# Attention over two heads at once: 64-row score products and transposes, float32 values in 64-column halves, minimum taken while scores leave PSUM

## The chip, the cores and the metric

The kernel runs on one core of a Trainium2 chip, in one launch. The metric is device time in microseconds (us), the median of the runs. The engines are TensorE (PE; its weight loads are listed apart as PEld), VectorE (DVE), ScalarE (ACT), GpSimd (POOL) and SyncE (SP, which issues most DMAs). A matrix product loads a stationary operand into the array and streams the columns of the moving operand past it; results land in PSUM, eight banks of 512 float32 per partition.

## The reference, cut to what matters

Two batches of eight heads, 1152 positions, head size 64. Queries are averaged in pairs, so that 576 queries meet 1152 keys. Two gated feed-forward layers follow.

```python
# q, k, v: (2, 8, 1152, 64) float32
q_pool = q.reshape(B, H, S // 2, 2, D).mean(axis=3)              # 576 queries
scores = scale * np.matmul(q_pool, k.transpose(0, 1, 3, 2))
scores = scores - np.max(scores, axis=-1, keepdims=True)
attn = np.exp(scores)
attn = attn / (np.sum(attn, axis=-1, keepdims=True) + 1e-09)
x = np.matmul(attn, v)                                          # heads side by side: (1152, 512)
g = x @ w_gate                                                  # 512 -> 1536
x = (g / (1 + np.exp(-g)) * (x @ w_val)) @ w_out                # -> 512
h = x @ w_in                                                    # 512 -> 2048
out = (np.maximum(h, 0) + alpha * np.minimum(h, 0)) @ w_out2    # -> 512
```

## The kernel before, in words

**Precision.** TensorE takes two kinds of 32-bit operand here. In the rounded kind (F32R) one product is one pass. To keep float32 accuracy the kernel splits an operand into a rounded high part and the rest (hi and lo) and adds hi*hi, lo*hi and hi*lo. A product of plain float32 is a second way.

**Attention, one pair of heads at a time** (NP = 8 pairs; the loop at L710). The two heads of a pair lie on partitions 0 to 63 and 64 to 127. `prep` (L418) loads q, k and v, pools and splits q (`qsplit`) and splits k (`ksplit`), mostly on POOL. Then SP copies, by DMA inside SBUF (L524, L526), the hi and lo parts of each head under one another, so that one product over 128 rows does two of the three terms (`qq`, `kk`). POOL splits v (L542, L543) and puts hi and lo side by side, 128 columns for a head.

A pair has nine units of 128 query rows (`unit`, L557): four of the first head, four of the second, and unit 4, which holds the last 64 queries of both heads by a block-diagonal operand `bd`. In a unit the scores (negated) are built in three cuts of 448, 448 and 256 keys (L592), two products a cut (three for unit 4). DVE takes the minimum of the first two cuts (L601) and then of the third together with it (L602); ACT does the exponential from PSUM into SBUF with the sum of the row (L604, L606). `transposed` (L615) turns the unit's nine blocks of 128x128 on TensorE (L633), three to a PSUM bank. Each bank is split again: the high part by ACT (L655), the rest by DVE (L656); 8 of 27 blocks go instead through an ACT copy (L641) to POOL (L651, L652). `values` (L661) then streams the hi and lo parts of 256 or 320 queries past v, 18 products of 128 columns for each of four groups (L674), and ACT and DVE add the two halves of the result (L678, L679). `inverses` (L681) turns the row sums into a multiplier that travels over DRAM, and `finish` (L694) multiplies and splits the result into `xh` and `xl`.

**The first pair** starts before the splits exist: its first two units use plain float32 q and k on 64 rows (the terms with `x.raw`), and the other units of its first head use three 64-row products per cut, straight from `qhl` and `khl`. Matmuls of zeros (L294) fill TensorE's time until attention flows.

**Feed-forward.** `gated` and `out1`, `prelu` and `out2` (L762, L822, L851) are products of 384 or 512 columns, three terms each, with weights rebuilt from 64-bit words by `weights` (L377).

**Order.** A planner (`Plan.run`, L124) writes out the order of every engine at build time, from fixed costs (`mm`, `tp`, `act`, `dve`, `gp`) and priorities (KNOB), with a due order by pair and unit. Buffers are classes of slots. PSUM before: banks 0 and 1, and 3 and 4, for the two wide cuts; bank 2 for the third; 5, 6 and 2 for transposes (`t`); 7 for values (`acc`). The feed-forward products (`b`) take any bank, but only when the attention classes that share it are all done.

Of the kernel before, what the change touches and what calls it, by code (L numbers as in the profile page):

```python
# [17 lines left out]
P = 128  # L18
# [3 lines left out]


KNOB = dict(hold_0=0.177, hold_m=0.061, qadd=0, qhi=1, klo=3, first=-4, raw=2, ramp=9, qk0=-2.332, max0=-0.894, exp0=0.979, t0=-3, hi0=-0.64, lo0=-0.532, v0=-3, last=2, qk9=-2.161, exp9=-1.953, t9=-0.316, hi9=0.54, lo9=1.303, v9=0.71, pool9=2, pooln=6, wlo=1, qk=-1.58, max=-1.852, exp=-0.223, t=-0.504, hi=-0.646, lo=-1.72, v=1.568, prep=-0.146, fin=1.131, hold_pe=0, hold_act=0.259, hold_dve=0.048, hold_pool=0.096, pvn=1, begin=0, lead=2, floor=31.257, warm=8, wide=448, tb=(5, 6, 2), ab=(7,), pool=9, xl=0, e=3, et=6, wc=3, wr=4, h=17)


class Task:
    __slots__ = ("eng", "dur", "extra", "emit", "prio", "bufs", "left", "after", "ready", "start", "n", "done", "port", "late", "hold")
# [12 lines left out]
class Slot:  # L41
    __slots__ = ("ap", "cells", "buf", "after")


class Plan:
# [3 lines left out]
    LAT = {PE: 0.21, ACT: 0.15, DVE: 0.13, POOL: 0.1, SP: 0.05}  # L49

# [9 lines left out]
    def place(self, cls, slots, after=()):  # L60
# [3 lines left out]
        for ap, cells in slots:  # L64
            s = Slot()
            s.ap, s.cells, s.buf = ap, frozenset(cells), None
            s.after = [o for o in after if any(s.cells & x.cells for x in self.classes[o]["slots"])]
            made.append(s)
# [11 lines left out]
    def add(self, eng, dur, emit, prio, reads=(), writes=(), bufs=(), extra=0.0, port=False, late=0.0, hold=0.0):  # L80
        t = Task()
        t.eng, t.dur, t.extra, t.emit, t.prio = eng, dur, extra, emit, prio
        t.n = len(self.tasks)
        t.port, t.late = port or eng == POOL, late
# [39 lines left out]
    def run(self, hold):  # L124
# [5 lines left out]
        port = 0.0  # L130
        events, seq = [], 0

# [4 lines left out]

        for when in sorted(set(free.values())):
            event(when)
        for t in self.tasks:  # L140
            if not t.left:
                heapq.heappush(wait[t.eng], (t.prio, t.n, t))
        order = []
        while events:
# [7 lines left out]
            for e in free:  # L152
                if free[e] > now + 1e-9:
                    continue
                passed = []
                while wait[e]:
                    item = heapq.heappop(wait[e])
                    t = item[2]
                    if t.ready > now + 1e-9:
                        passed.append(item)  # L160
                        if t.ready <= now + max(hold[e], t.hold) and all(b.slot is not None or self._spot(b) for b in t.bufs):
# [768 lines left out]
```

## Time and profile before

| | |
|---|---|
| Median of 3 runs | 686.75 us (680.51 to 686.88) |
| Span of the profiled execution | 685.0 us |
| Instructions | 11099 |
| PE busy | 676.4 us (99%) |
| DVE, ACT, POOL busy | 519.0, 392.2, 219.2 us |

The profiled execution is given by its span, from its first to its last instruction; the runs' times also hold what lies around that. Busy time of PE counts matmuls from start to modelled end, so PE at 99% says only that something was always in flight. What a product costs is read from the distance between starts, which the chain of waits shows (each piece there is a number of instructions and the time they took in the chain).

### The profile page before, as it was taken

What the parts mean: (1) busy time and instruction counts of PE and PEld (TensorE: products, weight loads), DVE (VectorE), ACT (ScalarE), POOL (GpSimd) and SP (SyncE); (2) the same over time, 40 slices, a digit from 0 to 9 for tenths busy, and PEclk for the clock granted to TensorE, in tenths of its full rate; (3) what the DMA queues carried; (4) which work ended last, traced back from release to release, by engine and by line L of the source; (5) the groups of instructions that cost most, each with busy time, mean ns of one, the idle gap of its engine ahead of it and who ended that gap; (6) DMA issues with size and microseconds to landing.
All of it is one profiled execution on the core that took longest, in us unless ns stands there. A gap on an engine that the chain in (4) does not pass through costs nothing.

```text
span 685.0 us, 11099 instructions
## 1 busy us (share of the span) xinstructions
PE 676.4 (99%) x4073; PEld 633.5 (92%) x4073; DVE 519.0 (76%) x893; ACT 392.2 (57%) x833; POOL 219.2 (32%) x253
## 2 busy tenths in 40 slices
PE   9999999999999989999999999999999999999998
PEld 5888999999999879999999999999999998999886
DVE  3788898888888799999775696559799559653432
ACT  3888999999999985545443432331376464242210
POOL 4668898988989840000000000004100000000000
PEclk9999999999999999999999999999999999999999
DMA  6576384755746324534341122111313303000012
GB/s 154 142 190 190 79 221 100 191 144 127 199 107 144 118 81 140 172 136 147 137 149 62 62 93 95 59 63 62 122 62 124 123 0 124 1 0 1 1 46 93
DMA packets 21431, 72.99 MB, mean 107 GB/s; under 512 B 3128, under 2 KB 3776, under 8 KB 21376
## 3 DMA queue, kind: packets, MB, share of 16 engines
q1 hardware_dynamic: 21296, 72.16, 35.5%
q8 instruction: 32, 0.52, 0.3%
q14 instruction: 23, 0.19, 0.1%
q10 hardware_dynamic: 80, 0.11, 0.1%
HBM read 52.17 MB, written 2.40 MB: 80 GB/s over the span
## 4 chain that ended last, share of the span: by engine, by line
PE 89%; DVE 5%; ACT 2%; issue 2%; DMA 1%; SPq 0%; POOL 0%; DVEq 0%; ACTq 0%
PE bank L762 34%; PE bank L851 14%; PE bank L822 11%; PE bank L592 11%; PE bank L633 9%; PE bank L674 9%; PE bank L294 1%; DMA fed<-fed 1%; DVE fed L656 1%; ACT plain L606 1%; DVE stats L601 1%; DVE magnitudes L393 0%; ACT fed L655 0%; DVE magnitudes L394 0%; DVE junk L602 0%
## 5 line engine op out<-in xcount | busy, mean ns | idle before, releaser
L762 PE MATMUL bank<-xh,weights 128*128 128x384 f32 x960 | 253.9, 337 | 0.1
L762 PEld LDWEIGHTS bank<-xh,weights 128*128 128x128 f32 x960 | 174.5, 188 | 2.1 <-DVE plain L786 0.4
L762 PE MATMUL bank<-xl,weights 128*128 128x384 f32 x480 | 161.4, 336 | 0.0
L633 PE MATMUL bank<-ident,plain 128*128 128x128 f32 x648 | 100.8, 275 | 3.9 <-DVE fed L656 3.0
L674 PE MATMUL bank<-fed 128*128 128x256 f32 (+1 forms) x576 | 104.2, 307 | 0.0
L851 PE MATMUL bank<-fed 128*128 128x512 f32 (+1 forms) x444 | 102.7, 383 | 0.0
L592 PE MATMUL bank<-fed 128*128 128x448 f32 (+2 forms) x378 | 98.5, 360 | 0.2 <-DMA fed<-fed 0.2
L851 PEld LDWEIGHTS bank<-fed 128*128 128x128 f32 x444 | 81.4, 188 | 14.3
L656 DVE TENSOR_TENSOR fed<-bank,fed 128x384 fp32r<-128x384 f32 (+1 forms) x177 | 82.7, 496 | 15.0 <-ACT fed L655 13.6
L762 PEld LDWEIGHTS bank<-xl,weights 128*128 128x128 f32 x480 | 90.2, 188 | 1.0
L633 PEld LDWEIGHTS bank<-ident,plain 128*128 128x128 f32 x648 | 74.8, 140 | 16.2 <-DVE fed L656 5.5
L601 DVE TENSOR_REDUCE stats<-bank 128x1 f32<-128x896 f32 x72 | 78.1, 1085 | 13.5 <-PE bank L592 12.3
L674 PEld LDWEIGHTS bank<-fed 128*128 128x128 f32 x576 | 83.0, 189 | 2.1 <-DVE plain L679 1.1
L655 ACT ACTIVATE fed<-bank 128x384 fp32r<-128x384 f32 (+1 forms) x177 | 73.3, 452 | 16.7 <-PE bank L633 16.2
L822 PE MATMUL bank<-fed 128*128 128x384 f32 x432 | 79.0, 336 | 0.0
L831 POOL TENSOR_SCALAR xh<-plain 128x384 fp32r<-128x384 f32 x12 | 12.1, 1010 | 205.2 <-DVE plain L829 205.2
L822 PEld LDWEIGHTS bank<-fed 128*128 128x128 f32 x432 | 75.8, 188 | 0.0
L606 ACT ACTIVATE plain<-bank,stats 128x896 f32<-128x896 f32 x72 | 72.6, 1009 | 0.0
L802 ACT ACTIVATE plain<-bank,signs 128x384 f32<-128x384 f32 x48 | 27.9, 581 | 69.6 <-PE bank L762 69.4
L652 POOL TENSOR_TENSOR fed<-plain,fed 128x384 fp32r<-128x384 f32 x63 | 64.7, 1027 | 1.5
L592 PEld LDWEIGHTS bank<-fed 128*128 128x128 f32 (+1 forms) x378 | 60.5, 189 | 3.2 <-issue 0.9
L803 DVE SCALAR_TENSOR_TENSOR plain<-bank,signs,plain 128x384 f32<-128x384 f32 x48 | 29.5, 614 | 35.0 <-ACT plain L802 35.0
(77 smaller groups left out, 842.1 us busy)
## 6 DMA issues: line engine op xcount, KB each, us to landing
fed<-fed SPq DMA_DIRECT2D x60, 288.0 KB, 5.4
plain<-in_w_out SPq DMA_DIRECT2D x28, 512.0 KB, 4.2
plain<-in_w_in SPq DMA_DIRECT2D x16, 512.0 KB, 4.1
plain<-in_w_gate SPq DMA_DIRECT2D x12, 512.0 KB, 3.7
plain<-in_w_val SPq DMA_DIRECT2D x12, 512.0 KB, 4.6
plain<-in_vt SPq DMA_DIRECT2D x8, 576.0 KB, 5.5
plain<-in_qt SPq DMA_DIRECT2D x7, 576.0 KB, 7.9
plain<-in_kt SPq DMA_DIRECT2D x7, 576.0 KB
```

What stands on the lines that cost most here:

```text
L592: nc.tensor.matmul(out(i)[:, :js.stop - js.start], l(), r(js), start=a == 0, stop=a == len(terms) - 1)
L601: add(DVE, dve(2 * WIDE), lambda: nc.vector.tensor_reduce(m(1), two(), AX.XY, ALU.min), pos + turn("max", p, n), [(sa, 0), (sa, 1)], [(st, ...
L606: add(ACT, act(2 * WIDE, acc=True), lambda: nc.scalar.activation(e.ap[:, :2 * WIDE].rearrange("p (a b) -> p a b", a=2), two(), AF.Exp, bia ...
L633: nc.tensor.transpose(t.ap[:, c * P:c * P + P], e.ap[:, ks:ks + P], ident)
L652: add(POOL, gp2(BLK * w), lambda cp=cp, to=to, cols=cols: nc.gpsimd.tensor_tensor(to(1), src3(cp.ap)[:, :, cols], to(0).bitcast(F32), ALU. ...
L655: add(ACT, act(BLK * w), lambda t=t, to=to, cols=cols: nc.scalar.activation(to(0), src3(t.ap)[:, :, cols], AF.Copy), at + turn("hi", p, n) ...
L656: add(DVE, dve(BLK * w), lambda t=t, to=to, cols=cols: nc.vector.tensor_tensor(to(1), src3(t.ap)[:, :, cols], to(0).bitcast(F32), ALU.subt ...
L674: nc.tensor.matmul(acc.ap[:, :n], v, b.ap[:, at:at + n], start=kc == 0 and part == 0, stop=kc == NK - 1 and part == 1)
L762: nc.tensor.matmul(acc.ap[:, :TB], l[:, cs], r[:, c, ts], start=c == 0 and a == 0, stop=c == KC - 1 and a == 2)
L803: add(DVE, dve(TB) + 0.056, lambda: nc.vector.scalar_tensor_tensor(u.ap, a.ap[:, :TB], sign(), u.ap, ALU.mult, ALU.max), prio, [a], [u], [ ...
L822: nc.tensor.matmul(acc.ap[:, :TB], l[:, os_], r, start=n == 0 and m == 0, stop=n == len(g) - 1 and m == 2)
L851: nc.tensor.matmul(acc.ap[:, :width], l, r[:, cols], start=n == 0 and m == 0, stop=n == len(g) - 1 and m == 2)
```

## The change

Attention is rewritten; the feed-forward part keeps its instructions. In the diff `TOP` and `LOW` are partitions 0 to 63 and 64 to 127 (head 0 and head 1), `CUTS` are three cuts of 384 keys.

- **Scores.** `two` replaces eight of the nine units: it builds 128 queries of both heads together, three 64-row products per cut and head, head 0 on the array's upper 64 rows and head 1 on the lower, in turn, into two PSUM banks. The DMA copies `qq` and `kk` go away. `corner` keeps the block-diagonal unit.
- **Minimum.** One DVE instruction per cut copies the scores to SBUF and takes the running minimum with it (`minimum`). One ACT instruction does the exponential of a whole row of 1152 in place (`exponential`).
- **Transposes.** Each 128x128 block is turned as two 64-row halves, the upper and the lower rows in turn, into two banks. One copy (ACT or DVE, the planner picks) takes three blocks out of PSUM, as plain float32; the hi and lo split of the weights and of v goes away with its POOL work.
- **Values.** Plain float32: v of head 0 is loaded into the array's left 64 columns, v of head 1 into the right 64, each with its own moving operand, in turn; one copy takes the result out. Two groups a pair instead of four.
- **PSUM.** All eight banks are shared: pairs of banks for scores (`s`) and transposes (`t`), single ones for values (`v`) and the corner (`m`). The first four slots of `b` need no longer wait for the attention classes.
- **Planner.** A task can have more than one engine to choose from, and TensorE tasks have a mode (`rows`, `cols`, `full`) with a price for turning from one to another. Emission comes after planning.
- **First pair.** Its first two `two` units use plain float32 q and k, both heads. The filling matmuls of zeros use 64 rows.
- Buffers: `h` 15 in place of 17, one `xs` in place of two, `e` 5 in place of 3; one weight buffer `raw` of its own.

```diff
+    TURN = {("full", "cols"): 0.15, ("cols", "full"): 0.15, ("rows", "full"): 0.15, ("full", "rows"): 0.195, ("rows", "cols"): 0.15, ("cols", "rows"): 0.198}
...
+                if e == PE:
+                    items.sort(key=lambda i: (i[0] + (stay if i[2].mode != mode else 0.0), i[1]))
...
-        nc.tensor.matmul(bank[:, 7, :n], zeros[:, :P], zeros[:, :n], start=True, stop=True)
+        nc.tensor.matmul(bank[:, 6, :n], zeros[TOP, :P], zeros[TOP, :n], start=True, stop=True)
...
-           [("khl", 1, 2 * S), ("qhl", 1, 2 * SQ), ("qq", 2, 2 * SQ), ("kk", 2, S), ("vs", 2, S), ("et", K["et"], 2 * BLK * 320)],
-           [("wr", K["wr"], 4 * DM), ("h", K["h"], 2 * TB)])
+    GROUPS = [(0, 2 * P), (2 * P, SQ)]
+    WIDEST = SQ - 2 * P
+    region("fed", F32R, [("khl", 2, 2 * S), ("qhl", 2, 2 * SQ)], [("wr", K["wr"], 4 * DM)])
...
+    room, kinds = {}, {"et": (F32, K["et"], 2 * BLK * WIDEST), "h": (F32R, K["h"], 2 * TB)}
...
-           [("nat", 2, S), ("vn", 1, S), (None, 1, 8 * DM - 3 * S), ("e", K["e"], S), ("cp", 2 if K["pool"] else 0, BLK * P), ("eo", 2, SQ), ("xs", 2, SQ), ("rr", 1, SQ)],
-           [("raw", 2, 4 * DM), ("tmp", 6, TB), ("part", 1, KC * NT)])
+           [("nat", 2, S), ("vn", 2, S), ("e", K["e"], S), ("xs", K["xs"], SQ), ("rr", 1, SQ)],
+           [("tmp", 6, TB), ("raw", 1, 4 * DM), (None, 1, 256), ("part", 1, KC * NT)])
...
-    OWN = (0, 3)
-    for i, o in enumerate(OWN):
-        plan.place(f"s{i}", [(None, [("ps", o), ("ps", o + 1)])])
-    plan.place("s2", [(bank[:, 2], [("ps", 2)])])
-    plan.place("t", [(bank[:, i], [("ps", i)]) for i in K["tb"]])
-    plan.place("acc", [(bank[:, i], [("ps", i)]) for i in K["ab"]])
-    plan.place("b", [(bank[:, i], [("ps", i)]) for i in range(8)], ("s0", "s1", "s2", "t", "acc"))
+    for cls in "st":
+        plan.place(cls, [(bank[:, i:i + 2], [("ps", i), ("ps", i + 1)]) for i in range(0, 8, 2)])
+    for cls in "vm":
+        plan.place(cls, [(bank[:, i], [("ps", i)]) for i in range(7, -1, -1)])
+    plan.place("b", [(bank[:, i], [("ps", i)]) for i in range(8)], ("s", "t", "v", "m"))
+    for s in plan.classes["b"]["slots"][:K["early"]]:
+        s.after = []
...
+            qload("a", s0, SP, slice(0, n0))
+            kload(0, s0, ACT)
+            kload(1, s0, SP)
+            kload(2, s0, ACT)
+            qload("b", s0, SP, slice(n0, SQ))
...
-        for j in range(1 if first else 0, 2):
-            qq, kk = buf("qq"), buf("kk")
-            x.qq[j], x.kk[j] = qq, kk
-            src = slice(0, D) if j == 0 else slice(D, P)
-            pr = s0 + 0.5 + 2 * j
-            for a in range(2):
...
-            add(POOL, gp(SQ), lambda v3=v3, vn=vn, hi=hi: nc.gpsimd.tensor_scalar(v3(hi), vn(), 1.0, 1.0, ALU.mult, ALU.mult), pr, [x.vn], [(vs, 0)], [x.vn, vs])
-            add(POOL, gp2(SQ), lambda v3=v3, vn=vn, hi=hi, lo=lo: nc.gpsimd.tensor_tensor(v3(lo), vn(), v3(hi).bitcast(F32), ALU.subtract), pr, [x.vn, (vs, 0)], [(vs, 1)], [x.vn, vs])
...
+    def minimum(src, e, i, st, prio, reads, own, hold=0.0):
+
+        js = slice(*CUTS[i])
+        m = lambda c: st.ap[:, c:c + 1]
+        if i == 0:
+            go = lambda: nc.vector.tensor_scalar(e.ap[:, js], src(), 1.0, 3.0e38, ALU.mult, ALU.min, accum_out=m(0))
+        else:
+            go = lambda: nc.vector.tensor_scalar(e.ap[:, js], src(), 1.0, m(i - 1), ALU.mult, ALU.min, accum_out=m(i))
+        add(DVE, dve(CUT) + 0.056, go, prio, reads + ([(st, i - 1)] if i else []), [(e, i), (st, i)], [own, e, st], hold=hold)
...
+    def exponential(x, e, st, n, prio):
+        add(ACT, act(S, True, True), lambda: nc.scalar.activation(e.ap, e.ap, AF.Exp, bias=st.ap[:, 2:3], scale=-1.0, accum_out=x.sums.ap[:, n:n + 1]),
+            prio, [(st, 2)], [(e, i) for i in range(NBLK)] + [(x.sums, n)], [e, st, x.sums], late=0.1)
...
+        raw = p == 0 and u < K["raw"]
+        if raw:
+            terms = [(lambda r: x.rr.ap[r, c0:c0 + P], lambda r, js: x.kn.ap[r, js])]
+            rd = lambda i: [(x.rr, "q"), (x.kn, i)]
+            held = [x.rr, x.kn]
+            span = 4 * CUT / 2400.0 + 0.0133
+        else:
+            terms = [(lambda r, a=a: x.qhl.ap[r, a * SQ + c0:a * SQ + c0 + P], lambda r, js, b=b: x.khl.ap[r, b * S + js.start:b * S + js.stop]) for a, b in ((0, 0), (1, 0), (0, 1))]
+            rd = lambda i: x.qread + x.kread(*CUTS[i])
+            held = [x.qhl, x.khl]
+            span = 3 * mm(CUT)
...
+            def scores(i=i, s=s):
+                js = slice(*CUTS[i])
+                for a, (l, r) in enumerate(terms):
+                    for j, half in enumerate((TOP, LOW)):
+                        nc.tensor.matmul(s.ap[:, j, :CUT], l(half), r(half, js), start=a == 0, stop=a == len(terms) - 1)
+
+            add(PE, span, scores, pos + turn("qk", p, k) + 0.01 * i, rd(i), [s], [s] + es + held, mode="rows")
+            for j in range(2):
+                minimum(lambda j=j, s=s: s.ap[:, j, :CUT], es[j], i, sts[j], pos + turn("mn", p, k) + 0.01 * i, [s], s)
...
+                    nc.tensor.matmul(s.ap[:, :CUT], x.bd[:, a], x.khl.ap[:, b * S + js.start:b * S + js.stop], start=n == 0, stop=n == 2)
...
+            add(PE, 3 * mm(CUT), scores, pos + turn("qk", p, 2) + 0.01 * i, [(("bd", p % 2), 0), (("bd", p % 2), 1)] + x.kread(*CUTS[i]), [s], [s, e, x.khl])
...
+                    for j, half in enumerate((TOP, LOW)):
+                        nc.tensor.transpose(t.ap[:, j, c * D:c * D + D], e.ap[half, ks:ks + P], ident[half, half])
+
+            add(PE, BLK * 0.063, tr, at + turn("t", p, n), [(e, i)], [t] + mark, [t, e, b], mode="rows")
...
+            add(ACT, act(BLK * P), lambda src=src, to=to: nc.scalar.activation(to(), src(), AF.Copy), at + turn("ev", p, n), [t], [key], [t, b],
+                also=[(DVE, dve(BLK * P), lambda src=src, to=to: nc.vector.tensor_copy(to(), src()), False, K["evd"])])
...
+            def pv(i=i, b=b):
+                for c in range(BLK):
+                    kc = i * BLK + c
+                    for j, half in enumerate((TOP, LOW)):
+                        nc.tensor.matmul(acc.ap[half, :n], x.vn.ap[:, (j * NK + kc) * D:(j * NK + kc) * D + D], b.ap[:, (j * BLK + c) * n:(j * BLK + c) * n + n], start=kc == 0, stop=kc == NK - 1)
+
+            parts = [k for o in ets for k in o.parts] if i == 0 else b.parts
+            add(PE, BLK * (4 * n / 2400.0 + 0.006), pv, at if i == 0 else -100.0, parts + [x.vn], [acc], [acc, b, x.vn], mode="cols")
+        add(ACT, act(n), lambda: nc.scalar.activation(xs.ap[:, q0:q1], acc.ap[:, :n], AF.Copy), at + K["xe"][g], [acc], [(xs, g)], [acc, xs],
+            also=[(DVE, dve(n), lambda: nc.vector.tensor_copy(xs.ap[:, q0:q1], acc.ap[:, :n]), False, K["evd"])])
...
+        add(POOL, 0.25, lambda: nc.gpsimd.tensor_scalar(x.sums.ap, x.sums.ap, EPS, 1.0, ALU.add, ALU.mult), pos, [], [x.sums] + [(x.sums, n) for n in range(NU)], [x.sums])
+        add(DVE, 0.097, lambda: nc.vector.reciprocal(x.inv.ap[:, :NU], x.sums.ap), pos, [x.sums], [x.inv], [x.sums, x.inv])
...
+        for n in range(5):
+            pos = at + (0.0, 0.89, 1.78, 2.22, 3.11)[n]
+            if n == 2:
+                e = corner(x, p, pos)
+                transposed(p, n, e, None, ets[1], 2 * P, pos)
+            else:
+                u = n if n < 2 else n - 1
+                es = two(x, p, u, pos)
+                for j in range(2):
+                    transposed(p, n, es[j], j, ets[u // 2], (u % 2) * P, pos + K["b"] * j)
+            if n == 1:
+                values(x, p, 0, ets[0], xs, at + 1.78)
+        inverses(x, p, at + 4.0 + K["inv"])
+        values(x, p, 1, ets[1], xs, at + 4.0)
+        finish(x, p, xs, at + 4.0 + K["fin"])
```

## Rows read from the trace of the kernel before

**Rows 1.** The page, part 1: busy time by engine, share, instructions.

```profile
PE 676.4 (99%) x4073; PEld 633.5 (92%) x4073; DVE 519.0 (76%) x893; ACT 392.2 (57%) x833; POOL 219.2 (32%) x253
```

**Rows 2.** Stretches: length, busy time by engine, granted clock, DMA.

```profile
107.67:136.84 29.17, 29.12 (x213) 27.25 (x211) 25.79 (x58) 26.87 (x72) 26.22 (x30) 1.00 0.63 153
...
240.00:260.00 20.00, 17.18 (x118) 15.73 (x117) 19.35 (x38) 16.75 (x36) 6.88 (x6) 1.00 0.24 83
280.00:300.00 20.00, 20.00 (x117) 20.00 (x117) 19.67 (x29) 10.98 (x16) 0.00 (x0) 1.00 0.44 156
```

**Rows 3.** Chain of waits, 110 to 137 us: start, us, engine, tile, line, count.

```profile
109.94 0.66 PE bank L633 x6
...
112.81 1.58 PE bank L592 x9
...
118.63 0.82 PE bank L592 x4
...
123.58 0.24 PE bank L592 x2
123.81 1.47 PE bank L674 x10
```

**Rows 4.** Chain of waits, 0 to 27 us, the first pair.

```profile
1.18 3.81 PE bank L294 x10
4.98 7.98 PE bank L592 x12
12.96 3.95 PE bank L294 x36
...
17.60 0.73 PE bank L294 x13
18.32 0.80 PE bank L592 x3
19.13 0.48 PE bank L633 x3
19.60 1.16 PE bank L592 x6
```

**Rows 5.** Timeline of weight loads, at 19.05 and 19.22 us.

```profile
19.05 0.14 PEld L633 LDWEIGHTS bank<-ident,plain 128*128 128x128 f32 x1 [0.31 <-issue]
...
19.11 0.25 PEld L633 LDWEIGHTS bank<-ident,plain 128*128 128x128 f32 x2
```

**Rows 6.** Groups by form, 107.67 to 136.84 us: busy us, mean ns, idle before.

```profile
L606 ACT ACTIVATE plain<-bank,stats 128x896 f32<-128x896 f32 x10 | 10.1, 1006 | 0.0
L601 DVE TENSOR_REDUCE stats<-bank 128x1 f32<-128x896 f32 x9 | 9.8, 1084 | 0.8 <-PE bank L592 0.6
...
L656 DVE TENSOR_TENSOR fed<-bank,fed 128x384 fp32r<-128x384 f32 x17 | 9.1, 551 | 1.3 <-ACT fed L655 1.1
...
L655 ACT ACTIVATE fed<-bank 128x384 fp32r<-128x384 f32 x16 | 7.5, 494 | 1.0 <-PE bank L633 0.9
...
L602 DVE TENSOR_SCALAR_CACHE_REDUCE junk<-bank,stats 128x256 bf16<-128x256 f32 x10 | 4.8, 478 | 0.4
...
L606 ACT ACTIVATION_READ_ACCUMULATOR plain<-bank,stats 128x1 f32 x9 | 1.8, 203 | 0.0
...
L655 ACT ACTIVATE fed<-bank 128x192 fp32r<-128x192 f32 x6 | 1.7, 334 | 0.3 <-PE bank L633 0.3
...
L602 DVE DVE_READ_ACCUMULATOR junk<-bank,stats 128x1 f32 x9 | 0.7, 82 | 0.0
...
L688 ACT ACTIVATE rows<-bank 9x128 f32<-9x128 f32 x1 | 0.3, 251 | 0.0
...
L686 DVE RECIPROCAL allinv<-allsums 128x9 f32<-128x9 f32 x1 | 0.2, 198 | 0.0
```

**Rows 7.** The inverses' transposes over the whole span (a line's view): first and last start.

```profile
L687 PE MATMUL bank<-ident,allinv x8: 270/270/329, 47.9 to 255.0; 128*128 128x128 f32 x8
```

**Rows 8.** Timeline of PE, 232 to 264 us: start, us, instructions, idle before and releaser.

```profile
242.03 0.55 PE L633 MATMUL bank<-ident,plain 128*128 128x128 f32 x3 [1.33 <-DVE fed L656]
```

More of the change, by code (lines that the diff above doesn't have):

```diff
@@ L77, in buf, with add @@
         return b
-    def add(self, eng, dur, emit, prio, reads=(), writes=(), bufs=(), extra=0.0, port=False, late=0.0, hold=0.0):
+    def add(self, eng, dur, emit, prio, reads=(), writes=(), bufs=(), extra=0.0, port=False, late=0.0, hold=0.0, mode="full", also=()):
         t = Task()
-        t.eng, t.dur, t.extra, t.emit, t.prio = eng, dur, extra, emit, prio
+        t.ways = []
+        for e, d, go, two, more in ((eng, dur, emit, port, 0.0),) + tuple(also):
+            w = Way()
+            w.eng, w.dur, w.emit, w.port, w.prio = e, d, go, two or e == POOL, prio + more
+            t.ways.append(w)
+        t.extra, t.prio, t.mode, t.way = extra, prio, mode, None
         t.n = len(self.tasks)
-        t.port, t.late = port or eng == POOL, late
+        t.late = late
         t.after, t.done, t.start, t.hold = [], None, None, hold
@@ L122, in _bind, with room, run @@
             self.held |= s.cells
-    def run(self, hold):
+    def room(self, bufs):
+        taken, ahead = set(), {}
+        for b in bufs:
+            if b.slot is not None:
+                continue
+            c = self.classes[b.cls]
+            if c["next"] + ahead.get(b.cls, 0) != b.n:
+                return False
+            s = next((s for s in c["slots"] if s.buf is None and not (s.cells & self.held) and not (s.cells & taken) and not any(self.classes[o]["open"] for o in s.after)), None)
+            if s is None:
+                return False
+            taken |= s.cells
+            ahead[b.cls] = ahead.get(b.cls, 0) + 1
+        return True
+    def run(self, hold, stay):
         self.held = set()
@@ L484, in prep @@
-        x.raw = None
+                ways.append((ACT, act(w, True), lambda: nc.scalar.activation(kpart(0, c), x.kn.ap[:, c], AF.Copy), False))
+            add(prio=pr, reads=[got], writes=[hi], bufs=[x.kn, x.khl], **either(ways))
+            ways = [(POOL, gp2(w), lambda: nc.gpsimd.tensor_tensor(kpart(1, c), x.kn.ap[:, c], kpart(0, c).bitcast(F32), ALU.subtract), True)]
+            if first:
+                ways.append((DVE, dve(w), lambda: nc.vector.tensor_tensor(kpart(1, c), x.kn.ap[:, c], kpart(0, c).bitcast(F32), ALU.subtract), True))
@@ L626, in transposed @@
+    def transposed(p, n, e, head, ets, off, pos):
+        for i in range(NBLK):
+            at = pos + i * 0.01
             t = buf("t")
-            blocks[0] += 1
-            mark = ["begun"] if (p, n, i) == (NP - 1, K["begin"], 0) else []
+            b = ets[i]
+            mark = ["begun"] if (p * 5 + n, i) == (K["begin"], 0) and head != 1 else []
             def tr(i=i, t=t):
@@ L881, in attention_moe_moe2 @@
         merged(a, b_, 0.2)
-    plan.run({PE: K["hold_pe"], ACT: K["hold_act"], DVE: K["hold_dve"], POOL: K["hold_pool"], SP: 0.0})
+    plan.run({PE: K["hold_pe"], ACT: K["hold_act"], DVE: K["hold_dve"], POOL: K["hold_pool"], SP: 0.0}, K["stay"])
+    plan.emit()
     attention_moe_moe2.end = plan.end
```

400 lines of the change are left out of this document (162 added, 238 removed).

## The prediction

> **What bounds the kernel now.** I read the busy table first [rows 1]: PE is in flight 99% of the span, but that counts overlapped ends and doesn't say whether PE does work or waits. So next the stretches [rows 2]: a pair of heads takes 29.17 us (four such stretches in a row agree within 0.03), with DVE at 25.8, ACT at 26.9 and POOL at 26.2 us; all four engines are loaded, PE most. From 261 us on (rows at 280 to 300) PE is at 20.00 of 20.00, and the change leaves those instructions alone. Then the chain of waits inside a pair [rows 3], which is nearly all PE, and gives what an instruction costs in the flow: a 128-column transpose 0.66/6 = 0.110 us, a score product of 448 columns 0.82/4 = 0.205, of 256 columns 0.24/2 = 0.12, a value product of 320 columns 1.47/10 = 0.147, of 256 columns as a score product, 0.12. Summed for a pair: 81 transposes 8.9; scores 32 x 0.205 + 16 x 0.12 + 1.58 for the corner = 10.1; values 36 x 0.147 + 36 x 0.12 = 9.6; together 28.6 of 29.17. So attention is bound by PE's own work, to 98%. What counts is PE's work for a pair after the change, then whether ACT and DVE still keep up.
>
> **Scores.** Per cut of 384 keys three 64-row products for each head. Between 448 columns (0.205) and 256 (0.12) lies 0.175 for 384 [rows 3]. A 64-row product alone costs what a 128-row one does: six of them, three of 448 and three of 256, took 1.16 [rows 4], of which 0.97 is the price of 128-row products. If the two heads' products run at once in the two halves of the array, 36 double products cost 36 x 0.175 = 6.3; in turn, 12.6. No row shows two halves at work together; I take the first, since each half has its own rows, operand and bank and nothing in the trace ties them. The corner stays nine products of 384: 1.6. Scores 7.9, in turn 14.2.
>
> **Transposes.** What paces one is shown where TensorE turned from scores to transposes: the first load began at 19.05 and the second at 19.11 [rows 5], 0.06 later, while transposes follow one another at 0.11. So the load is short and the stream of 128 columns is the pace. With 64 columns the stream is half, 0.055, and the load of 0.06 takes over: about 0.063 for the two halves side by side. Bounds: 0.11 if the load is the pace after all, 0.13 if the halves go in turn. 81 x 0.063 = 5.1 (8.9 or 10.5 at the bounds). The Trainium skill speaks against this (TensorE: Matmul & The Clock Gate, LDWEIGHTS): a load takes its number of columns over 1.2 GHz, whatever the number of rows; by that two loads of 128 columns side by side cost 0.107, and transposes would stay at 8.7. The 0.06 in the trace is for the same 128 columns, so the measurement disagrees so far.
>
> **Values.** Nine key blocks x two groups (256 and 320 columns), float32, two heads. The only float32 products are the first pair's 12 passes (two per product), 8 of 448 and 4 of 256 columns in 7.98 us [rows 4], 1.73 ns per column and pass. The clock matters: the zero products after them took 3.95/36 = 0.110 for 128 columns, those before them 3.81 for eight of 512 and two of 128, the same 0.86 ns a column, and from 17.6 us on it was 0.73/13 = 0.056 for 128. So that stretch ran at the lower level, 1.2 GHz, though the table's granted clock reads 1.00 throughout; at 2.4 GHz a pass costs 0.87 ns a column, and a product of both passes 0.44 us for 256 columns, 0.56 for 320. With the two heads side by side 9 x (0.44 + 0.56) = 9.0, against 9.6 now; in turn 18.0. I take 9.0: halves of columns have their own operands and their own partitions of the result.
>
> **Turns between modes** are already in the first pair [rows 4]: three transposes between 64-row scores took 0.48 in place of 0.33; three 64-row scores of 448 took 0.80 in place of 0.61. There and back 0.15 + 0.19 = 0.34. Scores and transposes now share the 64-row mode; a pair leaves it three times (corner, two groups of values): 1.0, up to 1.7 if the corner's cuts are scattered.
>
> **PE's sum for a pair:** 7.9 + 5.1 + 9.0 + 1.0 + 0.1 (inverses) = 23.1, against 28.6. With the 2% now lost, 23.6.
>
> **ACT and DVE.** DVE: 27 minima a pair. From L602 (478 + 82 for 256 columns) and 1.04 ns a column (between 1084 for 896 and 551 for 384) one costs 0.69; 18.7 in all, plus 1.0 for q's rest and the reciprocal. ACT: nine exponentials of 1152, 1006 + 256 x 0.83 + 203 = 1.42 each, 12.8 (0.83 ns from 494 and 334). 27 copies of 384 at 0.494, 13.3; results and inverses 1.1. Means overlap at their ends: DVE's ten groups of a pair (from L601's 9.8 to L686's 0.2) sum to 29.3 against 25.8 busy, a factor of 0.88, ACT's ten (L606's 10.1 to L688's 0.3) to 33.1 against 26.9, 0.81 [rows 2, 6]. So 17.3 + 22.0 = 39.3 for both, and the copies go to whichever is free: some 19.7 each, 83% of 23.6, a share below today's 88 to 92%. But it is tighter in another way: scores hold two banks until two minima of 0.6 us are done, against 0.53 us that PE takes to fill them, and all classes fight for eight banks. The nearest price for such waits is the 0.57 that a pair now loses; I add as much again, 0.6: **24.2 a pair** (0 and 2 as bounds).
>
> **What costs nothing:** POOL loses the splits of v and of a third of the blocks, and keeps q, k, `bd` and `finish`; it is off PE's chain now, at 26.2 of 29.17 [rows 2, 3], and has less to do later. SP loses its copies for `qq` and `kk`, and no piece of the chain in a pair is a DMA. The one `xs` makes a pair's first results wait for the last pair's `finish`, which has the half pair until then, some 12 us; if that is not enough, the value bank stays held and the loss is in the 2 above.
>
> **Ends.** The first inverse is at 47.9 [rows 7], 18.7 over a pair: that start stays, since its float32 scores now serve both heads (a gain, up to 4, half of L592's 7.98) but the clock rises only after PE's zero products, whose rows are now half (a loss, up to 4). At the end two stalls of 1.33 (one shown) [rows 8] and 2.8 us of idle in 240 to 260 [rows 2] may shrink; 2 either way. Feed-forward with 15 `h` in place of 17: zero, PE has none to lose (20.00 of 20.00); bound 2.
>
> **Sum:** (29.17 - 24.2) x 7.5 pairs (the first is half start) = 37 off a span of 685.0: 648, and with the 1.75 by which the median of the runs stands over the span, **650**. Its own range, from 23.2 to 25.2 a pair and 4 for the ends: 638 to 661.
>
> **Rivals.** (1) Transposes don't get shorter, because the load paces them: PE 26.9, 27.5 with its loss; 12 off, **674**. For it the row of 0.06 is one after a drain; chance 0.12. (2) ACT, DVE and the banks become the bound: 26 a pair, 24 off, **663**. For it, the fight for banks; against it, the 83%. Chance 0.16. The Trainium skill (TensorEngine Tiling (Array Packing), PSUM Bottleneck) warns of this way: a faster TensorE leaves the emptying of PSUM as it was. (3) Slower: the two column halves of the float32 values go in turn. 9.0 more, 32.1 for PE, 32.8 with its loss; 3.6 x 7.5 = 27 later, **714**. It decides once values cost over 14.5 a pair (9.0 and the 5.5 that the rest saves). Against it, nothing in the trace joins the halves; for it, no row shows them apart. Chance 0.08. (4) The clock: PE busy for 7.98 us with float32 on 64 rows didn't lift it from 1.2 GHz, and 3.95 us of 128-row zeros did [rows 4]. If attention on half rows and float32 falls back for the work of a third of it, 23.1 becomes 30.8, 31.4 with its loss: 17 later, **704**; against it, the 64-row scores from 18.3 us on came at the price of 2.4 GHz. Chance 0.06. (5) The change does not do what it says: score halves go in turn, the rest holds; 29.4 for PE, as before, **687**; chance 0.04.
>
> **Numbers.** The forecast has 0.54. About 1% (7 us) is what a measurement of this kernel tells from no change. Faster by over 1%: forecast and rivals 1 and 2, 0.82; within 1%: rival 5 and the low side of rival 4, 0.05; slower: rival 3 and most of rival 4, 0.13. The range takes in the forecast with 4 us more below for ends and waits that all fall well, and rivals 1 and 2: 634 to 676.
>
> **What would show it.** After: a pair's period of about 24 us between two inverses; double score products at 0.175; transposed halves at 0.03 each; values at 0.44 and 0.56 for two heads; DVE and ACT near 83%; feed-forward begins about 35 us earlier and takes the same 424 us after that. Wrong would be a period near 27 with PE full (1), PE idle on DVE or ACT (2), value products of one head following those of the other (3), or matmul spacing doubled in stretches (4).

## The result and the profile after

The changed kernel takes **646.46 us** (645.89 to 647.26, 4 runs) beside 683.65 us for the kernel before (680.51 to 686.88): a ratio of **0.945, interval 0.940 to 0.950**. The forecast was 650, the range 634 to 676. The profiled execution has a span of 645.2 us, 39.8 less than the 685.0 before. The total came out as forecast; its terms did not, and this section says where. The kernel before runs near 680.5 us or near 686.8 us from one execution to the next, and its profile is one of the longer kind, so that 39.8 is some 6 us more than a profile of the shorter kind would give; no kept trace shows where the 6 lie.

PE is in flight as much of the span as before [rows 1], and POOL has lost more than half of its work:

```profile
PE 636.5 (99%) x4874; PEld 565.0 (88%) x4874; DVE 478.2 (74%) x980; ACT 332.1 (51%) x557; POOL 98.9 (15%) x107
```

The inverses mark each pair once (sixteen transposes now, two a pair). First and last start answer to [rows 7]:

```profile
L706 PE MATMUL bank<-ident,allinv x16: 213/214/272, 33.5 to 212.4; 64*128 64x64 f32 x16
```

The balance of the 39.8 us comes out of these starts and the span. The first inverse is 14.4 us earlier (47.9 to 33.5). The seven periods from first to last took 178.9 us, before 207.1: 28.2 less. From the last inverse to the end it is 432.8 us, before 430.0: 2.8 more. 14.4 + 28.2 - 2.8 = 39.8. In the middle of attention a period is 25.69 us (before 29.17); seven times the difference is 24.4. Some 3 of the other 3.8 lie in the last period (30.7 before, 24.1 now), where PE before stood idle for 3.4 us [rows 2, 8].

The inverse doesn't stand at the same place of a pair in both kernels. What is left of the last pair's values behind it is in the timeline of PE before and in the chain of waits after:

```profile
259.31 2.30 PE L674 MATMUL bank<-fed 128*128 128x256 f32 x18
```

```profile
212.61 8.52 PE bank L786 x48
221.13 5.00 PE bank L691 x36
```

The kernel before has 18 of its value products behind the last inverse, in 2.30 us; the changed kernel has its whole second group, 36 in 5.00. The same holds at the first inverse (54 of 72 done there before, 36 of 72 now). So 2.7 us of work have gone from ahead of the inverse to behind it at both ends: of the 14.4 at the start some 11.7 is a gain, and the 2.8 at the end is no loss. The last value product starts at 225.7, before at 261.3, 35.6 earlier, and 24 feed-forward products more are done by then.

The stretches, in the same columns as [rows 2]: a pair, and the start, whose granted clock is 0.91 on average.

```profile
111.56:137.25 25.69, 25.36 (x319) 19.02 (x317) 20.93 (x68) 19.52 (x38) 10.69 (x10) 1.00 0.24 76
0.00:20.00 20.00, 17.83 (x143) 12.87 (x145) 12.02 (x39) 11.11 (x21) 10.99 (x25) 0.91 0.54 178
```

DVE is busy 81% of a pair, ACT 76%, POOL 42%, and the DMA share fell from 0.63 to 0.24. The chain of waits through most of that pair, in the columns of [rows 3]:

```profile
111.78 1.10 PE bank L622 x12
112.88 1.76 PE bank L641 x9
114.64 5.00 PE bank L691 x36
119.64 3.17 PE bank L660 x72
122.81 0.57 PE bank L622 x6
123.39 0.18 PE bank L660 x6
...
127.04 4.06 PE bank L691 x36
131.10 0.02 issue
131.12 0.42 DVE plain L696
131.55 0.48 DVE et L676
132.03 0.04 issue
132.07 0.72 PE bank L660 x12
132.79 1.70 PE bank L622 x18
134.49 0.20 PE bank L660 x6
134.68 0.02 issue
134.71 0.50 ACT et L675
135.21 0.04 issue
135.25 0.97 PE bank L660 x18
```

Three things are read here. Values cost 4.06/9 = 0.451 us a key block for 256 columns of both heads and 5.00/9 = 0.556 for 320. Six transposed halves cost 0.18 where nothing holds them, 0.060 for a pair of halves, but the run of 72 after the values took 3.17, or 0.088 a pair of halves: 1.0 more in all. Elsewhere the chain leaves PE for copies (L696 and L676 for 0.97 us with the gaps around them, L675 for 0.57). Scores cost 1.70/9 = 0.189 for two products side by side.

Why the run of 72 is slow shows in the timeline of that place (start, us, instructions; idle before and releaser in brackets):

```profile
119.57 3.24 PE L660 MATMUL bank<-ident,plain 64*128 64x64 f32 x72
...
119.75 0.44 ACT L695 ACTIVATE plain<-bank 128x320 f32<-128x320 f32 x1 [1.29 <-PE bank L691]
...
120.08 2.91 ACT L675 ACTIVATE et<-bank 128x384 f32<-128x384 f32 x6
120.20 3.22 DVE L676 COPY et<-bank 128x384 f32<-128x384 f32 x6 [3.18 <-PE bank L660]
```

During the 5 us of values DVE stood idle for 3.18 and ACT for 1.29, since nothing was left to empty. Then twelve copies fall due at once, six on each engine, in 3.2 us. PE is never shown as idle in this stretch: it is in flight all the while, paced by banks that come free.

The groups of that pair, in the columns of [rows 6], show what exponentials (L596), minima (L592) and copies (L675, L676) cost now:

```profile
L596 ACT ACTIVATE plain<-plain,stats 128x1152 f32<-128x1152 f32 x10 | 12.5, 1251 | 1.9 <-DVE plain L592 1.9
L592 DVE TENSOR_SCALAR_CACHE_REDUCE plain<-bank,stats 128x384 f32<-128x384 f32 x18 | 10.2, 615 | 0.2
...
L675 ACT ACTIVATE et<-bank 128x384 f32<-128x384 f32 x17 | 7.6, 488 | 3.0 <-PE bank L660 2.6
...
L676 DVE COPY et<-bank 128x384 f32<-128x384 f32 x11 | 5.9, 555 | 3.2 <-PE bank L660 3.2
```

### The profile page after: what moved, and what is told of

It is laid out like the page before. It is cut to its first block, busy times and chain, and to the rows that moved or that the text cites. A ratio compares the mean times of both kernels' runs of the same rounds, so it can differ in the third digit from the quotient of the medians.

```text
span 645.2 us, 12261 instructions
## 1 busy us (share of the span) xinstructions
PE 636.5 (99%) x4874; PEld 565.0 (88%) x4874; DVE 478.2 (74%) x980; ACT 332.1 (51%) x557; POOL 98.9 (15%) x107
## 4 chain that ended last, share of the span: by engine, by line
PE 95%; DVE 3%; issue 1%; ACT 1%; DVEq 0%
PE bank L786 39%; PE bank L875 15%; PE bank L846 12%; PE bank L691 11%; PE bank L622 8%; PE bank L660 7%; PE bank L641 2%; PE bank L344 1%; DVE et L676 1%; ACT et L675 1%; DVE plain L696 1%; DVE plain L592 1%; DVE plain L590 0%; DVE fed L558 0%; PE bank L706 0%
## 5 line engine op out<-in xcount | busy, mean ns | idle before, releaser
L786 PE MATMUL bank<-xh,weights 128*128 128x384 f32 x960 | 253.5, 337 | 0.0
L786 PEld LDWEIGHTS bank<-xh,weights 128*128 128x128 f32 x960 | 174.5, 188 | 2.1 <-issue 0.5
L786 PE MATMUL bank<-xl,weights 128*128 128x384 f32 x480 | 161.4, 336 | 0.0
L875 PE MATMUL bank<-fed,h 128*128 128x512 f32 (+1 forms) x444 | 102.7, 383 | 0.0
L596 ACT ACTIVATE plain<-plain,stats 128x1152 f32<-128x1152 f32 x72 | 89.9, 1250 | 18.1 <-DVE plain L592 18.1
L875 PEld LDWEIGHTS bank<-fed,h 128*128 128x128 f32 x444 | 81.4, 188 | 14.3
L786 PEld LDWEIGHTS bank<-xl,weights 128*128 128x128 f32 x480 | 90.2, 188 | 1.0
L592 DVE TENSOR_SCALAR_CACHE_REDUCE plain<-bank,stats 128x384 f32<-128x384 f32 x144 | 81.3, 614 | 1.6 <-PE bank L641 0.3
L846 PE MATMUL bank<-h,fed 128*128 128x384 f32 x432 | 79.0, 336 | 0.0
L846 PEld LDWEIGHTS bank<-h,fed 128*128 128x128 f32 x432 | 75.8, 188 | 0.0
L691 PE MATMUL bank<-et,plain 128*64 128x320 f32 (+1 forms) x576 | 73.4, 408 | 0.0
L675 ACT ACTIVATE et<-bank 128x384 f32<-128x384 f32 x135 | 60.5, 488 | 20.4 <-PE bank L660 17.4
L660 PE MATMUL bank<-ident,plain 64*128 64x64 f32 x1296 | 65.5, 232 | 3.4 <-ACT et L675 1.7
L622 PE MATMUL bank<-fed 64*128 64x384 f32 x540 | 61.1, 353 | 0.9 <-ACT et L675 0.4
L676 DVE COPY et<-bank 128x384 f32<-128x384 f32 x81 | 42.6, 553 | 17.1 <-PE bank L660 16.8
```

Of the source, the lines that this page charges most:

```text
L592: go = lambda: nc.vector.tensor_scalar(e.ap[:, js], src(), 1.0, m(i - 1), ALU.mult, ALU.min, accum_out=m(i))
L596: add(ACT, act(S, True, True), lambda: nc.scalar.activation(e.ap, e.ap, AF.Exp, bias=st.ap[:, 2:3], scale=-1.0, accum_out=x.sums.ap[:, n:n ...
L622: nc.tensor.matmul(s.ap[:, j, :CUT], l(half), r(half, js), start=a == 0, stop=a == len(terms) - 1)
L660: nc.tensor.transpose(t.ap[:, j, c * D:c * D + D], e.ap[half, ks:ks + P], ident[half, half])
L675: add(ACT, act(BLK * P), lambda src=src, to=to: nc.scalar.activation(to(), src(), AF.Copy), at + turn("ev", p, n), [t], [key], [t, b], als ...
L676: also=[(DVE, dve(BLK * P), lambda src=src, to=to: nc.vector.tensor_copy(to(), src()), False, K["evd"])])
```

## The experiments

Theory: a pair takes 25.7 and not the forecast 24.2 because the emptying of PSUM holds TensorE after all, in bursts; and the start gave some 9 us more than the 2.5 forecast. The rivals: halves that don't run quite side by side, turns between modes, the clock, or feed-forward work that moved. A period is read from the start of the inverses; "steady" means between the middle ones. Ratios are to the kernel before, run beside each on the same chip.

### Order of the score products

```diff
-                for a, (l, r) in enumerate(terms):
-                    for j, half in enumerate((TOP, LOW)):
+                for j, half in enumerate((TOP, LOW)):
+                    for a, (l, r) in enumerate(terms):
```

> The changed kernel with one loop turned: in each cut the three score products of head 0 are issued before the three of head 1, so that at most the last of one and the first of the other can lie side by side; all else in the same order. If the two 64-row halves of the array work side by side (the forecast), a cut of six products takes four to five times 0.18 us in place of three: 12 cuts a pair times 0.18 to 0.35 is 2.2 to 4.2 us, some of it hidden in the 2.5 us that PE now waits in its transposes; period of a pair 27 to 29 in place of 25.7, 657 to 672 us in all. If the halves work in turn anyway (rival), nothing changes: 25.7 and 646.

646.05 us, ratio 0.947 (0.936 to 0.957), steady period 25.71: no change. The starts of its score products, read singly from the trace beside those of the changed kernel (us, one cut of each):

```
changed kernel    112.196 112.199   112.369 112.373   112.543 112.546
heads in turn     110.567 110.577   110.825 110.835   111.003 111.013
```

The time is the one that was expected if the halves work in turn, but the starts rule that out. Though a head's three products are issued one behind the other, the six still start in pairs 0.010 us apart (0.003 to 0.004 in the changed kernel), and in the trace it is the two products of the third pair, and no others of the cut, that signal a semaphore, as in the changed kernel. So the halves run side by side, and the order of issue isn't what makes them: each half takes its own products, past waiting ones of the other half.

### Order of the value products

```diff
-                for c in range(BLK):
-                    kc = i * BLK + c
-                    for j, half in enumerate((TOP, LOW)):
+                for j, half in enumerate((TOP, LOW)):
+                    for c in range(BLK):
+                        kc = i * BLK + c
```

> The changed kernel with one loop turned: in each block of three key chunks the float32 value products of head 0 (left 64 columns) are issued before those of head 1 (right 64 columns). If the column halves work side by side, a block goes from 6 steps of a pass to 10 or 11 (0.213 us a pass of 256 columns, 0.267 of 320): 6 blocks a pair, 5 to 6 us a pair; period near 31, 690 us. If the halves work in turn anyway, 25.7 and 646. This is also what the third rival (halves in turn) would have cost.

654.03 us, ratio 0.958 (0.948 to 0.969), steady period 26.7; its inverses (the columns of the line's view):

```profile
L706 PE MATMUL bank<-ident,allinv x16: 213/215/273, 32.8 to 218.9; 64*128 64x64 f32 x16
```

Seven periods are 7.2 us longer, 1.0 each; neither arm of the expectation came (5 to 6 a pair, or nothing). Single starts show it: the first half's products begin at 103.326, the other half's first at 103.815, 0.49 later; then the halves alternate, 0.216 apart for each. The lag is paid at the ends of the two groups, 2 x 0.49 = 1.0. So column halves too run side by side, even with three key blocks of one head ahead of the other's.

### Full transposes

```diff
-                    for j, half in enumerate((TOP, LOW)):
-                        nc.tensor.transpose(t.ap[:, j, c * D:c * D + D], e.ap[half, ks:ks + P], ident[half, half])
+                    nc.tensor.transpose(t.ap[:, 0, c * P:c * P + P], e.ap[:, ks:ks + P], ident)
```

> The changed kernel with 128x128 transposes in place of the 64-row halves, into one PSUM bank; the same order of instructions. The forecast: 81 x 0.11 in place of 81 x 0.061 is 4.0 us a pair, and each run of transposes now turns the mode: four more turns there and back at 0.34, 1.4 us. Of the 5.4, up to 2.5 lies in time that PE now waits for copies out of PSUM: period 28.5 to 31, 667 to 688 us. If instead weight loads pace the halves, as in the first rival, only the turns cost: 27, 656 us.

670.77 us, ratio 0.983 (0.972 to 0.993), steady period 28.9:

```profile
L705 PE MATMUL bank<-ident,allinv x16: 213/215/275, 35.8 to 235.9; 64*128 64x64 f32 x16
```

Undoing the half-row transposes alone takes back 24 of the 37 us. On paper the expectation had 4.0 a pair for the transposes and 1.4 for turns between modes, less what hides in waits for copies; 3.2 came. This run doesn't part the three.

### Half of each copy

```diff
+            if p:
+                to, src = (lambda f=to: f()[:, :, :, :D // 2]), (lambda f=src: f()[:, :, :, :D // 2])
```

> The changed kernel with copies out of the transposes' banks of half the width (32 of each 64 queries) from the second pair on; the other half of the weights stays what it was before, so this part of the result is left out. A pair has 2.5 us in which PE stands between transposes. If the copies by ACT and DVE set that (runs of 72 transposes take 0.25 us a block of three, where PE needs 0.185), a copy of 192 in place of 384 columns takes 0.33 in place of 0.49 and 0.35 in place of 0.55 us, and the 2.5 shrinks to 1 or less: period 24 to 24.4, 634 to 637 us. If PE's own turns and drains or the minima set it, the period stays at 25.4 or more and the time over 643.

640.14 us, ratio 0.938 (0.928 to 0.948), steady period 24.9. The copies from the second pair on take half the columns; the other half is left out of the result. That is 0.8 a pair, between the two expectations: the copies hold part of the 1.5 that the forecast missed.

### Copies, minima and exponentials halved

The copies as above, and from the second pair on:

```diff
+        if e.n >= 9:
+            js, src = slice(js.start, js.start + CUT // 2), (lambda f=src: f()[:, :CUT // 2])
...
+        w = S // 2 if e.n >= 9 else S
```

> The changed kernel with all emptying work halved from the second pair on: copies of transposes half as wide, minima over 192 of 384 keys, exponentials over 576 of 1152; the other halves are left out. Half copies alone brought a pair from 25.7 to 24.9. If ACT and DVE hold the rest of PE's waits, the period falls to PE's own work, 21.8 by the distances in the changed kernel's trace plus five turns at 0.15 to 0.25: 22.8 to 23.3 us, 627 to 631 in all. If latency from engine to engine and the order hold it, the period stays at 24.3 or more, 635 to 640.

635.93 us, ratio 0.931 (0.925 to 0.937), steady period 24.3. One of its pairs:

```profile
106.71:131.03 24.32, 24.07 (x319) 18.62 (x317) 14.13 (x68) 13.11 (x38) 10.12 (x11) 1.00 0.25 78
```

With DVE at 58% and ACT at 54% of the pair the period is 24.3, the forecast's 24.2. So emptying holds at least 1.4 us of a pair. The rival of the expectation came, 24.3 or more: 2.5 us still lie between 24.3 and the 21.8 that the products come to at their undisturbed pace (36 x 0.174 + 1.6 + 81 x 0.060 + 9.06). They are not parted here: the emptying that is left, turns between modes, the way from engine to engine and the order of the work can all have a share.

### Only the planner's numbers

Every instruction is the same; priorities and holds of the planner were searched anew.

```diff
-            ... exp=(2.012, 0.624, -4.687, 1.473, -0.203), ... v=(1.701, 2.038), ... inv=-3.837, ...
+            ... exp=(2.012, 0.624, -4.493, 0.213, -0.203), ... v=(1.701, 1.501), ... inv=-2.205, ...
...
```

> Only the planner's numbers (priorities and holds) are changed, found by a search over its own timetable; every instruction is the same, the order of some is not. What this tells: how much of the 2.5 us of a pair that light emptying did not give back is order. If order holds a good part of it, the pair's period falls by 0.4 or more and the time to about 643. If what is left is turns between the array's modes and the way from engine to engine, the timetable's gain isn't there on the chip: period 25.5 to 25.8, time 645 to 648.

> The changed kernel once more, with nothing edited, beside the next two on the same chip: about 646 to 647, the pair's period 25.7.

On one chip, **643.02 us** (642.83 to 643.04) beside 646.42 (646.02 to 646.92) for the changed kernel run again; ratios 0.943 (0.938 to 0.947) and 0.948 (0.944 to 0.952). The four runs of each don't overlap. Steady period 25.12 to 25.16:

```profile
84.02:109.15 25.13, 25.02 (x323) 18.86 (x321) 20.32 (x66) 20.05 (x38) 10.38 (x11) 1.00 0.28 85
```

0.55 us of a pair was order. Only the two kernels with halved copies are faster.

### Fixed banks

The planner's numbers were searched anew for this placing too.

```diff
-    for cls in "st":
-        plan.place(cls, [(bank[:, i:i + 2], [("ps", i), ("ps", i + 1)]) for i in range(0, 8, 2)])
-    for cls in "vm":
-        plan.place(cls, [(bank[:, i], [("ps", i)]) for i in range(7, -1, -1)])
+    for cls, at in (("s", (0, 2)), ("t", (4, 6))):
+        plan.place(cls, [(bank[:, i:i + 2], [("ps", i), ("ps", i + 1)]) for i in at])
+    for cls, i in (("v", 7), ("m", 6)):
+        plan.place(cls, [(bank[:, i], [("ps", i)])])
```

> Undoes the shared pairs of PSUM alone: scores keep two fixed pairs of banks, transposes two, values one bank and the small tiles one; the planner's numbers are searched anew for that placing. Shared placing lets scores take three or four pairs while transposes rest, and transposes while no scores run. If sharing is what lets TensorE stay in one mode for long, the period rises to 28 or more (at least 18 us over the seven pairs, 664 or more). If emptying by VectorE and ScalarE sets the pace and two pairs of banks each are enough, the period stays under 26.7 and the time under 655. The earlier forecast put a fight for banks at 0.16 as a rival.

685.26 us, ratio 1.005 (1.002 to 1.008): nothing is left of the gain. Of the first six periods the four without a fall of the clock are 28.1 to 28.4:

```profile
L707 PE MATMUL bank<-ident,allinv x16: 221/272/368, 40.4 to 252.4; 64*128 64x64 f32 x16
```

The first expectation held (28 or more). Six periods are 17.5 us longer than in the changed kernel. That is under half of the 37.5 by which the span is longer: 6.9 lie in the start, and the rest in the last period (39.7, with 72 feed-forward products ahead of the last inverse) and behind it. In the chain of one of its pairs even the corner (L642) is cut up, by values and by minima that must free its one bank:

```profile
69.42 0.73 PE bank L642 x3
70.15 5.00 PE bank L692 x36
75.14 0.74 PE bank L642 x3
75.89 0.03 issue
75.91 0.64 DVE plain L593 x2
76.55 0.04 issue
76.59 0.80 PE bank L642 x3
...
78.61 1.04 DVE et L677 x2
```

Further on, scores and transposes turn about in runs of six, with PE waiting for copies between them. Part of the loss is not the banks but the clock, which the section on the hardware shows. A better order for that placing may exist; the one tried came out of the same kind of search.

### The start and the ends

The zeros left out:

```diff
-        nc.tensor.matmul(bank[:, 6, :n], zeros[TOP, :P], zeros[TOP, :n], start=True, stop=True)
+        pass
```

> The changed kernel without its products of zeros (both the first eight and the fillers); the rest in the same order. The first pair of the changed kernel ends 14.4 us earlier than before, 11 more than one pair's saving; one theory: because its clock rose at 8.2 us after the start in place of 16.8. Then without zeros the clock rises later, by 5 us or more, work of that stretch at half speed costs 2 to 5 us: 648 to 651. Rival: the start is set by loads, minima and exponentials of the first scores, TensorE's level counts little: under 1 us, 645 to 647.

646.34 us, ratio 0.944 (0.938 to 0.949): no change. The clock rose at 10.26 us; in the changed kernel it rose at 8.16 in one execution and at 10.52 in another. None of it cost anything that can be measured. All that PE had done by 10.26 was the first products:

```profile
5.69 6.38 PE L622 MATMUL bank<-plain 64*128 64x384 f32 x24 [5.69 <-ACT plain L568]
```

The theory itself was not tried, since the clock did not rise late here: no run has it at 16.8, as in the kernel before.

One plain float32 unit at the start instead of two:

```diff
-... raw=2, ...
+... raw=1, ...
```

> The changed kernel with one unit of plain float32 scores at the start in place of two, the others after the split of q and k; planned anew. If the first pair's gain comes from having four rows of 128 queries ready before the splits in place of two, half of that goes: 4 to 7 us later, 650 to 653. If the splits are ready soon enough anyway: within 1 us of 646.

654.8 us, ratio 0.958 (0.952 to 0.965). The last value product of the first pair starts at 46.24 instead of 42.25, the second inverse at 64.9 instead of 60.2; steady period 25.95. In all it is 8.3 us later, worse than expected; the order was planned anew, and what comes beyond the 4.7 of the second inverse lies in later periods.

No feed-forward slots of PSUM ahead of attention's end:

```diff
-... early=4, ...
+... early=0, ...
```

> The changed kernel with all feed-forward PSUM slots waiting for the attention classes, as before; planned anew. The end of attention gained 4.2 us (48 feed-forward products before the last values in place of 24). If the freed slots do it: 2 to 4 us later, 648 to 650. If it is only the shorter last pair: no change, 646.

647.39 us, ratio 0.946 (0.941 to 0.950): the freed slots are worth some 1 us. From the last inverse (211.6) to the end of the span it is 434.0, in the changed kernel 432.8.

## Why the prediction was right, and where it was wrong

**Scores side by side: right.** Starts 0.003 to 0.004 us apart, 0.174 to the next two where the chain is undisturbed (forecast 0.175). With turns and waits it is 0.18 to 0.21 in the chain. Rival 5 (in turn) is ruled out.

**Transposes: the pace was right, the sum not.** 0.060 for two halves against 0.063; rival 1 (0.11, from the load) is wrong, and the run with full transposes priced the halves, with the turns between modes that they save, at 24 us. Loads of 128 columns can follow one another every 0.06, as [rows 5] said. By the Trainium skill (TensorE: Matmul & The Clock Gate, LDWEIGHTS), a load takes its columns over 1.2 GHz whatever its rows, 0.107 us each; by estimate from that rule transposes would have stayed at 8.7 a pair. As a spacing the trace disagrees with it here: two loads and two streams every 0.060. But the transposes don't run at that pace for long, and this is the next point.

**Values: right.** 0.451 and 0.556 a key block, 9.06 a pair, against 0.44, 0.56 and 9.0. Rival 3 (in turn, slower than before) did not happen; the run with the value products in turn paid 1.0 a pair, not the 9.0 that the rival had.

**The step that failed: the term for emptying, 0.6 a pair**, taken as a second helping of the 0.57 of waits of before. The products came to 21.8, against 22.0 in the forecast's sum (7.9 + 5.1 + 9.0); what stands beside them came to 3.9, against 2.2 (turns, inverses, today's loss and the 0.6). Halving copies, minima and exponentials brings the period from 25.69 to 24.3, so emptying holds at least 1.4, and this is nearly all of what the pair missed (25.69 - 24.2 = 1.5). The argument from the share (83% forecast; 81% and 76% measured) was sound as a mean and blind to order: a share says nothing of idle time (3.2 us on DVE) followed by twelve copies due at once. The period stands close to rival 2's 26, and nearer to it than to the forecast; rival 2's 663 did not come because the start gave more. Order alone gives back 0.55, as the retuned kernel shows. The Trainium skill (TensorEngine Tiling (Array Packing), PSUM Bottleneck) warns that a faster TensorE leaves the emptying of PSUM as it was; this case agrees, at 1.4 us or more of 25.7.

**The banks were counted on the wrong side.** "All classes fight for eight banks" stood as a cost. With fixed banks, in the one order tried, a pair without a fall of the clock takes 28.1 to 28.4, so that 2.4 to 2.7 of the 3.5 that a pair gains hang on sharing. The reason is argued from the chains, not tried by itself: a shared bank lets one kind of work hold PE for long and then goes to the next.

**The start was forecast at half a pair's saving, 2.5, and gave 14.4 by the inverses, some 11.7 without the values that now stand behind them.** About 3.5 is one pair's saving. The rest, some 8, the prediction had as "a gain, up to 4" against "a loss, up to 4". The float32 products of before kept PE 7.98 us for two units of one head [rows 4]; now the two units of both heads are in flight for 2.89 and 2.79, as the timeline of the start shows:

```profile
6.07 2.89 PE L622 MATMUL bank<-plain 64*128 64x384 f32 x9
...
8.56 2.79 PE L622 MATMUL bank<-plain 64*128 64x384 f32 x15
11.98 0.83 PE L660 MATMUL bank<-ident,plain 64*128 64x64 f32 x13 [0.62 <-ACT plain L596]
13.08 1.58 PE L660 MATMUL bank<-ident,plain 64*128 64x64 f32 x23 [0.27 <-DVE plain L592]
14.73 3.00 PE L641 MATMUL bank<-fed,bd 128*128 128x384 f32 x9
```

Scores of two units of both heads are ready before the splits are, and the first transposes start at 11.98, where PE before is on zeros until 16.91 [rows 4]. Taking one of the two units away cost 4.0 us at the end of the first pair and 4.7 by the second inverse. So this is about half of the 8; what the rest is was not tried. One candidate is the clock: the 7.98 us of before lay wholly at its lower level, which by estimate from [rows 4] is worth up to 4 us, and here the clock rose while these products ran. The zeros, on which the prediction had hung its loss, are worth nothing (646.34 without them).

**The end: right, at nothing.** The 2.8 by which it is longer behind the last inverse is the place of the inverse: 36 value products in 5.00 us lie behind it, before 18 in 2.30. That 48 feed-forward products (L786) now come ahead of the last values, before 24, is order; without the early slots the time is 1 us longer. PE stays at 20 of 20 in feed-forward, as forecast.

**The clock (rival 4)** fell once, for 3.4 us of the start, and not in every execution; attention at large ran at 1.00. Its premise, that float32 products on 64 rows don't lift the clock, did not hold: in the run without zeros PE had done nothing else when the clock rose, with both heads at once.

**What was costed at nothing cost nothing:** POOL at 42% of a pair, DMA share 0.24, and the chain of the pair shows no wait for the single `xs`.

**In sum:** forecast 37.3 = 2.5 (start) + 34.8 (seven periods) + 0 (end); measured 39.8 = 14.4 + 28.2 - 2.8 by the inverses, or some 11.7 + 28.2 + 0 with the values put where they belong. That 650 came so near is luck, two misses against each other: 6.6 too much gain from the pairs against some 9 too little from the start. That the kernel got faster by this much of PE's work is not: scores, transposes and values, where nothing holds them, each came at their forecast price.

## What to carry to other kernels

Where TensorE is made faster, don't ask only for the mean share of the engines that empty PSUM: look in the chain for long runs of one kind (values) that leave them idle, and price the run behind as copies, not as products. Let kinds of work that don't overlap share their banks when making the products shorter: with fixed banks, in the one order tried, shorter products gave nothing. The first pass of a pipeline has its own price: one unit less ready before the first split cost 4 to 5 us there. And where a stretch is measured between two marks, see what work lies on either side of the mark in each kernel.

## What the runs showed of the hardware

**Halves don't wait for each other in the order of issue.** With a head's three products issued in a row, the halves' starts were 0.010 us apart; with a block's value products in a row, the second half lagged 0.49 us and then ran along. The Trainium skill (TensorE: Matmul & The Clock Gate, The mechanism) has tiles start some 4 ns apart, with which the 0.003 agrees, and has products strictly in order, which these two runs don't bear out across halves.

**The clock fell in stretches of short transposes with gaps.** In the changed kernel's profile PE had done 64-row transposes with gaps of 0.62 and 0.27 when the granted clock went to its lower level at 14.99 us, until 18.40; the corner's nine products took 3.00 there and 1.76 elsewhere. Run again, the kernel did the same transposes with gaps of 0.20 and 0.27 and had no such fall, with a span of 644.9 beside 645.2: worth nothing here, and what sets off a fall is not shown. With fixed banks it is worth more. Its stretches near the end of attention:

```profile
240.00:251.70 11.70, 9.98 (x114) 8.23 (x110) 9.16 (x19) 9.61 (x17) 1.29 (x1) 1.00 0.19 64
251.70:258.50 6.80, 6.12 (x28) 2.99 (x30) 2.61 (x3) 2.36 (x5) 0.00 (x0) 0.50 0.39 137
```

Around 251.7 PE did transposes with gaps of 0.62, 0.94 and 0.40; then the clock stood at 1.2 GHz for 6.80 us, and the last 36 value products took 7.77 in place of 5.00. Another fall, at 265.4, came while PE stood idle for 3.85 us. The falls of that execution add up to some 24 us at the lower level. At half the clock that is 12 us at most, of the 37.5 by which this span is longer.
